# Attention matmuls on the full 128x128 tile, and memory transposes for two heads at once, in an attention-plus-MLP kernel

## The chip, the cores and the metric

The kernel runs on one core of a Trainium2 chip. The metric is device time in microseconds (us) of one execution. A core has five engines that matter here: PE (TensorE: a weight load, in the profile PEld, followed by a matmul that streams the other operand past the weights), DVE (VectorE), ACT (ScalarE), POOL (GpSimd) and SP (SyncE, whose queue issues all DMAs of this kernel). Each engine executes its own queue of instructions strictly in the order in which the program wrote them; the queues meet at semaphores.

A matmul uses a tile of the array of rows*columns: rows is the length of the contraction (the partitions of both operands), columns is how many columns of weights are loaded. The profile writes this tile as 128*128, 64*128 (64 rows), 128*64 (64 columns) or 64*64.

## The reference

Attention for B, H, S, D = 4, 8, 576, 64, followed by two MLP layers on all 2304 tokens:

```
local   = softmax(causal(q k^T / 8)) v                      # 576 x 64 for each head
q_p     = elu(q) + 1
mem_out = (q_p M_prev) / (q_p z_prev + 1e-6)                # memory part, 576 x 64 for each head
attn    = g * mem_out + (1 - g) * local,  g = sigmoid(beta[h])
x       = attn, heads side by side: 2304 x 512
x       = (s * relu(x w_in)^2 + b) w_out                    # layer 1, d_ff = 2048
out     = leaky(x w_in2; alpha) w_out2                      # layer 2, d_ff = 2048
```

## The kernel before

**Stages.** Attention goes batch by batch (b = 0 to 3) and in a batch by pairs of heads (p = 0 to 3). A head's 576 queries are five chunks, `CHUNKS`: 64, 128, 128, 128, 128 queries; a chunk of index c sees 64 + 128c keys, so its last block of keys has 64, the others 128. Chunks 0 to 2 are one set, chunks 3 and 4 the other (`SETS`). For each chunk, `scores` (L469) computes the scores on PE (L627 or L673/L674), adds the mask and finds the maximum on DVE (L497), takes the exponential on ACT (L505); `turn` (L523) splits the weights into two float16 parts (ACT L551, DVE L555), sets the padding behind the last key to zero (POOL L559) and transposes them by a DMA (SP L564); `products` (L567) multiplies the transposed weights with the values (PE L584) into the bank `ob`.

**Two kinds of batch.** Batches 0 and 1 (`EXACT`) run `pair` (L609): float32 scores, and the products of the two heads go to rows 0 to 63 and 64 to 127 of one bank, so each product loads 64 columns of weights. Batches 2 and 3, the second half, run `head` (L655) twice for each pair: scores from float32r parts with two products (L673, L674), and value products with 128 columns (the high and the low part of the values), whose two halves of the bank are added at the end.

**Memory part.** `features` (L431) computes it for a pair of heads, queries on partitions, into the slot `sa` (PE L454, DVE L459 to L463). `remembered` (L589) transposes it on PE by a product with the identity matrix (L598) into the bank of the products. In `pair` it does so for both heads at once (128 columns); in `head` for the one head (64 columns), after the head's products of that set. Chunk 0 has 64 queries, so L598 uses 64 rows there. One float32 product of the program is two matmul instructions in the profile.

**End of a set in a head.** ACT scales one half of the bank into the output tile `xt` (L695), DVE adds the other half (L697). When both heads of a pair are through, `xt` goes to DRAM as `x1` (SP L719).

**Layers.** Layer 1 works on seven blocks of tokens (512, 320, 320 and four of 288), layer 2 on eight of 288. A block reads its rows of `x1` (SP L890, split by ACT L896 and DVE L898), and for each of 16 slices of d_ff does 12 matmuls of the first product (L800 to L802), the activation (ACT L814, L815, L822, DVE L823) and 12 of the second (L834 to L836). Block 0 needs batch 0, blocks 1 and 2 need batch 1, blocks 3 and 4 batch 2, blocks 5 and 6 batch 3. Blocks 0 to 4 are what PE can do beside the attention of batches 1 to 3.

**What sets the order.** `Plan` (L62) collects all operations with their reads, writes, priorities and written-out durations; `order` (L112) makes a list schedule: each engine takes the most urgent operation that is ready, attention (`ATT`) ahead of the layers (`MOE`). The result is one fixed queue for each engine. The written-out durations (`t_f`, `t_b`, `t_r`) depend on the streamed columns and not on the tile. Tenants of the pool of 15 slots (`Slot`) take a place when so many others are free as their reserve (`RES`) asks. Banks: from batch 1 on, scores, features and the like take S0 and S1 in turn (`next_bank`), products have the single bank O.

Of the kernel before, what the change touches and what calls it, by code (L numbers as in the profile page):

```python
# [18 lines left out]
# tokens of the blocks of the two layers: (first, tokens); layer 1's first takes both places of the operands  # L19
# [6 lines left out]
# query chunks: (first query, queries); a chunk sees the keys up to its last query  # L26
CHUNKS = [(0, 64), (64, 128), (192, 128), (320, 128), (448, 128)]
SETS = [(0, 1, 2), (3, 4)]
# chunks whose weights are transposed together
GROUPS = [[(0,), (1, 2)], [(3,), (4,)]]  # L30
NC = len(CHUNKS)
# [22 lines left out]
class Slot:  # L54
    """A tenant of the pool of equal slots; it gets its place when the operations are ordered."""
# [6 lines left out]
class Plan:  # L62
    """Operations in a logical order with what they read and write. order() is a list schedule
    of the graph: every engine takes, of the operations that are ready, the most urgent. A slot
    is taken by its first operation, if as many more are free as the slot's reserve asks, and
    is free again after its last."""
# [38 lines left out]
    def either(self, ways, **kw):  # L105
        """An operation for whichever of the engines comes to it first: ways is {engine: (duration, function)}."""
        eng = next(iter(ways))
        i = self.op(eng, *ways[eng], **kw)
        if len(ways) > 1:
            self.ways[i] = ways  # L110

    def order(self):  # L112
# [32 lines left out]
        def spot(t, s):  # L145
            """Where a slot could go: the last extra place, or else the one that has been free for longest."""
# [12 lines left out]
        while len(out) < n:  # L159
# [50 lines left out]
            if e == "PE":  # L210
                # at half the clock unless the last tick was busy enough
# [58 lines left out]
def build(tc, kd, kz, qd, vd, qp, mzd, beta8, sb2, win1, wout1, win2, wout2, alpha, outT):  # L270
# [7 lines left out]
    with tc.tile_pool(name="sb", bufs=1) as sb, tc.tile_pool(  # L278
# [5 lines left out]
        # the parts of a slice of d_ff: w_in's and w_out's; before they are there, the last slices' room serves as slots  # L284
# [13 lines left out]
        def cut(t, n, k, step=None):  # L298
            """The first n elements of the k-th part of t."""
            return t[:, k * (step or n):k * (step or n) + n]  # L300
# [27 lines left out]
        def at(s, n, dt=F32):  # L328
            """The first n elements of a slot, as dt."""
# [12 lines left out]
        # the last 128 columns: -8e9 where the key lies after the query  # L342
# [7 lines left out]
        def consts():  # L350
            # wsc = (1 + exp(beta)) / LIFT = 1 / ((1 - g) LIFT); bgc = 1 + exp(-beta) = 1 / g
            A.activation(out=wsc, in_=bsc, func=AF.Exp)
            A.activation(out=bgc, in_=bsc, func=AF.Exp, scale=-1.0)
# [14 lines left out]
        # the banks of MoE products serve the first batch's attention  # L368
# [8 lines left out]
        def gate(hg, ahead, ahead0):  # L377
            """A load for a head waits for the scores of an earlier one."""
# [3 lines left out]
        def either(kind, a_dur, a_fn, d_dur, d_fn, **kw):  # L382
            """An operation for the scalar or, of the kinds in FLEX, also for the vector engine."""
# [10 lines left out]
        # They are scaled by LIFT over the sum of their magnitudes, so that no part leaves float16's range.  # L394
        def values(b, p):
# [19 lines left out]
            # un = 1 / (scale LIFT)  # L415
# [53 lines left out]
        def scores(b, h, g, keys, scored):  # L469
            """keys: what the products read; scored: (rows, columns) -> the product's instructions."""  # L470
# [4 lines left out]
            for c in cs:  # L475
# [4 lines left out]
                # keys in one or two banks: (bank, column of maximum and sum, first key, keys)  # L480
# [10 lines left out]
                for bk, col, k0, kn in parts_s:  # L491
                    sp = bank_of[bk][0:nq, 0:kn]
                    dur, mm = scored(sp, q0, nq, k0, kn)
# [20 lines left out]
            # rows 64.. of chunk 0's column were set once and stay finite  # L514
# [8 lines left out]
        def turn(b, g, group, parts, turned):  # L523
            """group: what is transposed together, (head of the pair, chunk)."""
# [13 lines left out]
            for pw, c in group:  # L538
# [19 lines left out]
                # what is transposed with the chunk's last 64 keys has to be something; nothing uses it  # L558
# [8 lines left out]
        def products(g, part, parts, turned, sf, obk, ok, high, rows, first=False):  # L567
            """The products with the values: part (head of the pair, chunk) into rows of the bank. high: the high and
            low parts of the values go to the same rows, else the low ones follow in the next 64."""
# [6 lines left out]
            def mm():  # L576
                P = p_t()
                W = at(sf, 2 * NKB * 2 * D, FP16).rearrange("p (n h e) -> p n h e", h=2, e=2 * D)
                for kb in range(nkb):
                    kk = min(128, nk - kb * 128)  # L580
                    cols = [(slice(0, D), kb), (slice(D, 2 * D), kb), (slice(0, D), nkb + kb)] if high else [
                        (slice(0, 2 * D), kb), (slice(0, 2 * D), nkb + kb)]
                    for w, x in cols:
                        T.matmul(obk[rows, q0 - o0:q0 - o0 + nq], W[0:kk, kb, pw, w], P[0:kk, x, 0:nq],  # L584
# [4 lines left out]
        def remembered(g, heads, sa, obk, ok, rows, ch, first=True):  # L589
            """The memory part, transposed into the bank."""  # L590
# [3 lines left out]
            def mm():  # L594
                for c in cs:
                    q0, nq = CHUNKS[c]
                    F = at(sa, 2 * D * NC).rearrange("p (c e) -> p c e", c=NC)[0:nq, c, heads]
                    T.matmul(obk[rows, q0 - o0:q0 - o0 + nq], F, ident[0:nq, 0:nq], start=(first and c == cs[0]), stop=False,  # L598
# [402 lines left out]
```

## Time and profile before

| | us |
|---|---|
| median of 3 runs (lowest, highest) | 1096.52 (1095.52, 1099.56) |
| span of the profiled execution | 1099.4 |
| PE busy in it | 1073.4 (98%) |
| DVE busy | 684.6 (62%) |
| ACT busy | 529.8 (48%) |
| attention of batches 0 and 1, beside it block 0 from 105 on | 0 to 257 |
| attention of batches 2 and 3, beside it blocks 1 to 4 | 257 to 568 |
| rest of layer 1, layer 2 | 568 to 1099 |

The profile lists no device time of the profiled execution apart from its span, which lies at the upper end of the three runs. A PE line of the timeline gives the start of its first matmul, the time from there to the end of its last one, the line of the kernel, the tile, the form of the streamed operand and how many follow each other. Matmuls overlap, so what one costs in the queue is the time from its start to the start of the next line, not its own duration.

### The profile page before, as it was taken

To read this page: it belongs to the slowest core of one execution; us is meant where nothing else is said; L and a number is where in the kernel's file an instruction comes from. 1 tells how busy PE (TensorE), PEld (TensorE's weight loads), DVE (VectorE), ACT (ScalarE), POOL (GpSimd) and SP (SyncE) were. 2 spreads that over 40 slices of the span, in tenths; PEclk is the share of its full clock that TensorE was granted. 3 is DMA by queue.
4 is the path that set the end of the run, shared out by engine and by line. 5 is a ranking of instruction groups with operands and counts; after the bars stand their busy time and mean duration, and the time that the engine had idled before them with its cause. 6 is when DMAs were issued, how large, how long until landed. Compare 5 with 4: busy or idle time off the path is not lost.

```text
span 1099.4 us, 20528 instructions
## 1 busy us (share of the span) xinstructions
PE 1073.4 (98%) x7776; PEld 976.4 (89%) x7776; DVE 684.6 (62%) x1812; ACT 529.8 (48%) x1325; POOL 32.2 (3%) x171
## 2 busy tenths in 40 slices
PE   7978999999999999999999999999999999999998
PEld 5755777777889989989999999999999999999998
DVE  6768888867575566566646179984545454545443
ACT  7764666558576667668654466331212121212111
POOL 1100000000000000000000000000000000000000
PEclk9987999999999999999999999999999999999999
DMA  8899686665644564454434055321101010100000
GB/s 211 162 182 259 203 182 192 181 141 167 134 72 125 132 135 109 118 125 106 96 105 154 1 185 193 129 73 32 44 1 44 1 44 1 44 1 22 1 22 23
DMA packets 163860, 114.10 MB, mean 104 GB/s; under 512 B 127408, under 2 KB 141744, under 8 KB 163760
## 3 DMA queue, kind: packets, MB, share of 16 engines
q1 hardware_dynamic: 163760, 112.78, 39.1%
q8 instruction: 61, 1.00, 0.4%
q14 instruction: 39, 0.32, 0.1%
HBM read 68.19 MB, written 14.16 MB: 75 GB/s over the span
## 4 chain that ended last, share of the span: by engine, by line
PE 88%; DMA 5%; DVE 2%; issue 2%; ACT 2%; SPq 0%; POOL 0%; DVEq 0%; POOLq 0%; ACTq 0%
PE yb L834 12%; PE yb L836 12%; PE yb L835 12%; PE hb L800 8%; PE hb L802 7%; PE hb L801 7%; PE ob L584 7%; PE sp L800 3%; PE sp L801 3%; PE sp L802 3%; PE ob L598 2%; PE sp L627 2%; DMA pool<-pool 2%; PE ob L802 2%; PE ob L800 2%
## 5 line engine op out<-in xcount | busy, mean ns | idle before, releaser
L834 PE MATMUL yb<-gr,wt 128*128 128x288 f32 (+3 forms) x960 | 299.0, 311 | 0.9 <-ACT gr L822 0.9
L835 PE MATMUL yb<-gr,wt 128*128 128x288 f32 (+3 forms) x960 | 291.7, 304 | 0.0
L836 PE MATMUL yb<-gr,wt 128*128 128x288 f32 (+3 forms) x960 | 291.6, 304 | 0.0
L822 ACT CAST gr<-gt 128x288 fp32r<-128x288 f32 (+2 forms) x240 | 107.4, 447 | 305.4 <-DVE gt L820 297.0
L823 DVE TENSOR_TENSOR gr<-gt,gr 128x288 fp32r<-128x288 f32 (+2 forms) x240 | 114.2, 476 | 139.1 <-ACT gr L822 138.6
L800 PE MATMUL hb<-xr,wt 128*128 128x288 f32 (+2 forms) x576 | 186.1, 323 | 1.7 <-ACT gt L814 1.7
L834 PEld LDWEIGHTS yb<-gr,wt 128*128 128x128 f32 x960 | 181.0, 189 | 7.6 <-issue 2.1
L836 PEld LDWEIGHTS yb<-gr,wt 128*128 128x128 f32 x960 | 181.3, 189 | 3.6 <-DVE gr L823 0.8
L835 PEld LDWEIGHTS yb<-gr,wt 128*128 128x128 f32 x960 | 180.9, 188 | 2.0 <-issue 0.2
L802 PE MATMUL hb<-xr,wt 128*128 128x288 f32 (+2 forms) x576 | 178.6, 310 | 0.0
L801 PE MATMUL hb<-xr,wt 128*128 128x288 f32 (+2 forms) x576 | 178.6, 310 | 0.0
L800 PEld LDWEIGHTS hb<-xr,wt 128*128 128x128 f32 x576 | 108.8, 189 | 8.6 <-ACT gt L814 2.6
L801 PEld LDWEIGHTS hb<-xr,wt 128*128 128x128 f32 x576 | 109.0, 189 | 2.9 <-issue 0.6
L802 PEld LDWEIGHTS hb<-xr,wt 128*128 128x128 f32 x576 | 108.9, 189 | 3.0
L814 ACT ACTIVATE gt<-hb 128x288 f32<-128x288 f32 (+2 forms) x112 | 49.7, 444 | 106.8 <-PE hb L802 105.8
L505 ACT ACTIVATE pool<-sp,mx 64x64 f32<-64x64 f32 (+2 forms) x153 | 72.4, 474 | 35.4 <-DVE mx L497 27.2
L584 PEld LDWEIGHTS <-pool 64*64 64x64 f16 (+3 forms) x930 | 55.1, 103 | 38.1 <-issue 19.7
L497 DVE CUSTOM_DVE_ANT_0 sp<-sp,mask 64x64 f32<-64x64 f32 (+4 forms) x132 | 56.5, 438 | 42.6 <-PE sp L674 26.5
L584 PE MATMUL ob<-pool 128*128 128x128 f16 (+5 forms) x855 | 76.8, 221 | 4.1 <-DMA pool<-pool 4.0
L800 PE MATMUL sp<-xr,wt 128*128 128x288 f32 x256 | 75.5, 295 | 0.0
L801 PE MATMUL sp<-xr,wt 128*128 128x288 f32 x256 | 75.5, 295 | 0.0
L802 PE MATMUL sp<-xr,wt 128*128 128x288 f32 x256 | 75.4, 295 | 0.0
(174 smaller groups left out, 1694.1 us busy)
## 6 DMA issues: line engine op xcount, KB each, us to landing
pool<-win SPq DMA_DIRECT2D x19, 512.0 KB, 4.4
pool<-wout SPq DMA_DIRECT2D x17, 512.0 KB, 4.5
room<-wout SPq DMA_DIRECT2D x15, 512.0 KB, 4.3
room<-win SPq DMA_DIRECT2D x13, 512.0 KB, 4.3
pool<-qd SPq DMA_DIRECT2D x16, 288.0 KB, 3.1
pool<-kd SPq DMA_DIRECT2D x16, 288.0 KB, 3.7
pool<-y SPq DMA_DIRECT2D x16, 288.0 KB, 3.4
out_t<-pool SPq DMA_DIRECT2D x32, 144.0 KB, 1.8
```

What stands on the lines that cost most here:

```text
L497: op("DVE", t_dve(kn, 1.04, 0 if mk is None else 60), lambda sp=sp, nq=nq, mo=mo, kn=kn, mcol=mcol, last=last: V.tensor_tensor_reduce(out= ...
L505: op("ACT", t_act(kn, 50, 180), lambda sp=sp, p_c=p_c, k0=k0, kn=kn, mcol=mcol, scol=scol: A.activation(out=p_c()[:, k0:k0 + kn], in_=sp, ...
L584: T.matmul(obk[rows, q0 - o0:q0 - o0 + nq], W[0:kk, kb, pw, w], P[0:kk, x, 0:nq], start=(first and kb == x == 0), stop=False, skip_group_c ...
L800: T.matmul(H_, W_h, X_h, start=(d == 0), stop=False)
L801: T.matmul(H_, W_h, X_l, start=False, stop=False)
L802: T.matmul(H_, W_l, X_h, start=False, stop=(d == KD - 1))
L814: op("ACT", t_act(n, 50), lambda: A.activation(out=t_, in_=H_, func=AF.Relu), r=[hk, "gr"], w=[tk], prio=-1)
L822: op("ACT", t_act(n), lambda: A.copy(out=G_h, in_=t_), r=[tk], w=[("gh", gj)], prio=-1)
L823: op("DVE", t_dve(n), lambda: V.tensor_tensor(out=G_l, in0=t_, in1=G_h.bitcast(F32), op=ALU.subtract), r=[tk, ("gh", gj)], w=[("gl", gj)], ...
L834: T.matmul(Y, W_h, G_h, start=(f == 0), stop=False)
L835: T.matmul(Y, W_l, G_h, start=False, stop=False)
L836: T.matmul(Y, W_h, G_l, start=False, stop=(f == KF - 1))
```

## The change

Four edits, and the priorities that go with them (the diff also blanks comments, which moves nothing up to L490):

1. Chunk 0's scores load 128 columns of weights (queries 0 to 127) in place of 64; rows 64 to 127 of the result are not read.
2. The products with the last block of keys use all 128 rows; the padding is zero.
3. `remembered` uses all 128 rows, also for chunk 0, and always both heads.
4. In batches 2 and 3 `remembered` leaves `head`. A new `recall` does it once for each pair, ahead of the pair's scores, in a bank of the ring S0/S1, and ACT or DVE (whichever the schedule finds free) scales the result into `xt`. At the end of a set `head` then adds both halves of its bank to `xt` with two DVE operations; the ACT operation L695 is gone.

```diff
 # scores
+                    dur, mm = scored(bank_of[bk][:, 0:kn], q0, k0, kn)
                     sp = bank_of[bk][0:nq, 0:kn]
-                    dur, mm = scored(sp, q0, nq, k0, kn)
...
 # products
-                    kk = min(128, nk - kb * 128)
...
-                        T.matmul(obk[rows, q0 - o0:q0 - o0 + nq], W[0:kk, kb, pw, w], P[0:kk, x, 0:nq],
+                        T.matmul(obk[rows, q0 - o0:q0 - o0 + nq], W[:, kb, pw, w], P[:, x, 0:nq],
                                  start=(first and kb == x == 0), stop=False, skip_group_check=True)
...
-        def remembered(g, heads, sa, obk, ok, rows, ch, first=True):
+        def remembered(g, sa, obk, ok, prio):
...
-                    F = at(sa, 2 * D * NC).rearrange("p (c e) -> p c e", c=NC)[0:nq, c, heads]
-                    T.matmul(obk[rows, q0 - o0:q0 - o0 + nq], F, ident[0:nq, 0:nq], start=(first and c == cs[0]), stop=False,
+                    F = at(sa, 2 * D * NC).rearrange("p (c e) -> p c e", c=NC)[:, c]
+                    T.matmul(obk[:, q0 - o0:q0 - o0 + nq], F, ident[:, 0:nq], start=(c == cs[0]), stop=False,
                              skip_group_check=True)
...
 # pair
-                            T.matmul(sp, at(sqp, S)[:, q0:q0 + nq], at(s, S)[:, k0:k0 + kn], start=True, stop=True)
+                            T.matmul(sp, at(sqp, S)[:, q0:q0 + 128], at(s, S)[:, k0:k0 + kn], start=True, stop=True)
...
+        def recall(b, p, sa, xt):
+            j = p % 2
+            for g in range(len(SETS)):
+                ok = next_bank(b, "S")
+                obk = bank_of[ok]
+                remembered(g, sa, obk, ok, ATT + cnt["ch"] * 10 - 4)
+                o0, qn = span_of(g)
+                either("x", t_act(qn, 50, 93), lambda o0=o0, qn=qn, obk=obk: A.activation(
+                    out=at(xt, S)[:, o0:o0 + qn], in_=obk[:, 0:qn], func=AF.Copy, scale=vsc[:, j, 1:2]),
+                    t_dve(qn, 1.04, 60), lambda o0=o0, qn=qn, obk=obk: V.tensor_scalar(
+                    out=at(xt, S)[:, o0:o0 + qn], in0=obk[:, 0:qn], scalar1=vsc[:, j, 1:2], scalar2=None, op0=ALU.mult),
+                    r=[ok, ("un", j)], w=[(xt, odd, g) for odd in range(2)])
...
 # head
-                    T.matmul(sp, qh[:, q0:q0 + nq], ks[:, k0:k0 + kn], start=True, stop=False)
-                    T.matmul(sp, ql[:, q0:q0 + nq], ks[:, k0:k0 + kn], start=False, stop=True)
+                    T.matmul(sp, qh[:, q0:q0 + 128], ks[:, k0:k0 + kn], start=True, stop=False)
+                    T.matmul(sp, ql[:, q0:q0 + 128], ks[:, k0:k0 + kn], start=False, stop=True)
...
-                remembered(g, slice(D * odd, D * odd + D), sa, obk, ok, slice(r0, r0 + 64), ch0, False)
...
-                op("ACT", t_act(qn, 50, 93), lambda xr=xr, qn=qn, obk=obk: A.activation(
-                    out=xr(), in_=obk[r1:r1 + 64, 0:qn], func=AF.Copy, scale=un[r0:r0 + 64]), r=[ok, ("un", j)], w=[(xt, odd, g)])
-                op("DVE", t_dve(qn, 1.04, 60), lambda xr=xr, qn=qn, obk=obk: V.scalar_tensor_tensor(
-                    out=xr(), in0=obk[r0:r0 + 64, 0:qn], scalar=un[r0:r0 + 64], in1=xr(),
-                    op0=ALU.mult, op1=ALU.add), r=[("un", j)], w=[ok, (xt, odd, g)])
+                for r, w in ((r1, []), (r0, [ok])):
+                    op("DVE", t_dve(qn, 1.04, 60), lambda xr=xr, qn=qn, obk=obk, r=r: V.scalar_tensor_tensor(
+                        out=xr(), in0=obk[r:r + 64, 0:qn], scalar=un[r0:r0 + 64], in1=xr(),
+                        op0=ALU.mult, op1=ALU.add), r=[ok, ("un", j)], w=w + [(xt, odd, g)])
...
 # attention
-                    head(b, 2 * p, sa, sf, xt)
-                    head(b, 2 * p + 1, sa, sf, xt)
+                    recall(b, p, sa, xt)
+                    head(b, 2 * p, sf, xt)
+                    head(b, 2 * p + 1, sf, xt)
```

## Rows read from the trace of the kernel before

**Rows 1.** Stretches: length, busy us of PE, PEld, DVE, ACT, POOL, clock, DMA.

```profile
0.00:105.00 105.00, 87.67 (x606) 60.31 (x606) 78.88 (x296) 73.32 (x207) 10.15 (x59) 0.91 0.88 202
105.00:257.00 152.00, 151.27 (x877) 112.80 (x878) 121.08 (x320) 93.72 (x217) 7.29 (x32) 0.99 0.70 186
257.00:568.00 311.00, 308.01 (x2329) 277.95 (x2328) 193.73 (x588) 217.30 (x573) 14.77 (x80) 1.00 0.48 112
```

**Rows 2.** Waits in 257:568: who waited for whom, us in total, times, longest.

```profile
ACT gt L814 <- PE hb L802: 44.3, 35, 3.5
DVE sp L497 <- PE sp L674: 32.5, 41, 2.3
```

**Rows 3.** What L584 in 257:568 waited for: us, times.

```profile
  DMA pool<-pool: 2.0, 5
```

**Rows 4.** PE timeline, a head of batch 2, first set: start us, us, what.

```profile
310.16 0.31 PE L835 MATMUL yb<-gr,wt 128*128 128x322 f32 x1
310.30 0.30 PE L836 MATMUL yb<-gr,wt 128*128 128x322 f32 x1
310.54 0.23 PE L584 MATMUL ob<-pool 64*128 64x64 f16 x2
310.70 0.41 PE L800 MATMUL hb<-xr,wt 128*128 128x320 f32 x1
310.95 0.31 PE L801 MATMUL hb<-xr,wt 128*128 128x320 f32 x1
...
312.56 0.19 PE L673 MATMUL sp<-ks,qh 128*64 128x64 f32 x1
...
312.93 1.04 PE L584 MATMUL ob<-pool 128*128 128x128 f16 x10
313.91 0.91 PE L598 MATMUL ob<-ident,pool 64*64 64x64 f32 x6
314.75 0.42 PE L834 MATMUL yb<-gr,wt 128*128 128x322 f32 x1
```

**Rows 5.** PE timeline, the same head's chunk 4 and its memory part.

```profile
319.23 0.84 PE L584 MATMUL ob<-pool 128*128 128x128 f16 x10
320.00 0.65 PE L598 MATMUL ob<-ident,pool 128*64 128x128 f32 x4
320.58 0.40 PE L673 MATMUL sp<-ks,qh 128*128 128x288 f32 x1
```

**Rows 6.** The first seven matmuls of that chunk 4, all on the full tile.

```profile
319.23 0.56 PE L584 MATMUL ob<-pool 128*128 128x128 f16 x7
```

**Rows 7.** PE timeline in batch 1: memory transposes of both heads, full tile.

```profile
152.80 0.61 PE L598 MATMUL ob<-ident,pool 128*128 128x128 f32 x4
153.16 0.48 PE L800 MATMUL hb<-xr,wt 128*128 128x512 f32 x1
153.47 0.40 PE L801 MATMUL hb<-xr,wt 128*128 128x512 f32 x1
```

**Rows 8.** PE timeline in batch 1: chunk 4's products and what follows.

```profile
165.14 1.14 PE L584 MATMUL ob<-pool 128*64 128x128 f16 x15
166.21 0.50 PE L800 MATMUL hb<-xr,wt 128*128 128x512 f32 x1
```

**Rows 9.** The first twelve of those products, those with 128 rows.

```profile
165.14 0.86 PE L584 MATMUL ob<-pool 128*64 128x128 f16 x12
```

**Rows 10.** L697 in 257:568: length, DVE busy us, clock, DMA share, GB/s.

```profile
257.00:568.00 311.00, 15.98 (x31) 1.00 0.48 112
```

**Rows 11.** Form group in 257:568: products on the full tile: busy us, mean ns.

```profile
L584 PE MATMUL ob<-pool 128*128 128x128 f16 x320 | 28.9, 221 | 1.4 <-DMA pool<-pool 1.4
```

**Rows 12.** The last DMA into x1: start us, us, what.

```profile
568.99 0.33 SPq L719 DMA_DIRECT2D x<-pool  x1
```

**Rows 13.** The split of block 5's input, the first block after attention.

```profile
574.45 0.83 DVE L898 TENSOR_TENSOR xr<-pool,xr 128x288 fp32r<-128x288 f32 x2
```

**Rows 14.** The first matmul of block 5 on PE.

```profile
583.46 0.29 PE L800 MATMUL hb<-xr,wt 128*128 128x288 f32 x1
```

More of the change, by code (lines that the diff above doesn't have):

```diff
@@ L596, in mm @@
                     q0, nq = CHUNKS[c]
-                    F = at(sa, 2 * D * NC).rearrange("p (c e) -> p c e", c=NC)[0:nq, c, heads]
-                    T.matmul(obk[rows, q0 - o0:q0 - o0 + nq], F, ident[0:nq, 0:nq], start=(first and c == cs[0]), stop=False,
+                    F = at(sa, 2 * D * NC).rearrange("p (c e) -> p c e", c=NC)[:, c]
+                    T.matmul(obk[:, q0 - o0:q0 - o0 + nq], F, ident[:, 0:nq], start=(c == cs[0]), stop=False,
                              skip_group_check=True)
-            op("PE", sum(t_f(CHUNKS[c][1]) for c in cs), mm, r=[(sa, g), "ident"], w=[ok], prio=ATT + ch * 10)
+            op("PE", sum(t_f(CHUNKS[c][1]) for c in cs), mm, r=[(sa, g), "ident"], w=[ok], prio=prio)
         def span_of(g):
@@ L624, in pair, with scored @@
                 for odd in range(2):
-                    def scored(sp, q0, nq, k0, kn, s=sk[odd]):
+                    def scored(sp, q0, k0, kn, s=sk[odd]):
                         def mm():
-                            T.matmul(sp, at(sqp, S)[:, q0:q0 + nq], at(s, S)[:, k0:k0 + kn], start=True, stop=True)
+                            T.matmul(sp, at(sqp, S)[:, q0:q0 + 128], at(s, S)[:, k0:k0 + kn], start=True, stop=True)
                         return t_f(kn), mm
@@ L637, in pair @@
                             turn(b, g, [(odd, c) for c in group], parts, turned)
-                remembered(g, slice(0, 2 * D), sa, obk, ok, slice(0, 128), ch0)
+                remembered(g, sa, obk, ok, ATT + ch0 * 10)
                 for odd in range(2):
@@ L652, in pair, with head @@
                     r=[ok, ("un", j)], w=[(xt, odd, g) for odd in range(2)])
-        def head(b, h, sa, sf, xt):
+        def recall(b, p, sa, xt):
[10 more added lines that the diff above has]
+                    r=[ok, ("un", j)], w=[(xt, odd, g) for odd in range(2)])
+        def head(b, h, sf, xt):
             hg = b * H + h
@@ L669, in head, with scored @@
                 out=ql, in0=at(sq, S), in1=qh.bitcast(F32), op=ALU.subtract), r=[sq, "qh"], w=["ql"])
-            def scored(sp, q0, nq, k0, kn):
+            def scored(sp, q0, k0, kn):
                 def mm():
-                    T.matmul(sp, qh[:, q0:q0 + nq], ks[:, k0:k0 + kn], start=True, stop=False)
-                    T.matmul(sp, ql[:, q0:q0 + nq], ks[:, k0:k0 + kn], start=False, stop=True)
+                    T.matmul(sp, qh[:, q0:q0 + 128], ks[:, k0:k0 + kn], start=True, stop=False)
+                    T.matmul(sp, ql[:, q0:q0 + 128], ks[:, k0:k0 + kn], start=False, stop=True)
                 return 2 * t_r(kn), mm
```

## The prediction

> **What bounds the kernel now.** I read the busy shares by stretch first [rows 1]. From 257 to 568, the attention of batches 2 and 3, PE is busy 308.0 of 311 us, ACT 217.3, DVE 193.7. Busy time on PE does not by itself prove a bound, since matmuls overlap, so I looked next at who waits for whom there. ACT waited 44.3 us for the first product of the layers and DVE 32.5 us for scores [rows 2]; PE waited 2.0 us in all, five times, for the transposed weights [rows 3]. The queues are fixed, and PE's is the one that the others stand behind. Third, the PE timeline, start to start: what a switch of tile costs. From 105 to 257 PE is busy 151.3 of 152, DVE 121.1. From 0 to 105 PE is busy 87.7, its clock averages 0.91, so it ran in part at the lower of its two levels (1.2 and 2.4 GHz), and it waits there for loads and transposes [rows 1].
>
> **Prices.** A layer matmul of 322 columns takes 0.14 to 0.15 us from start to start from 310.16 to 310.30 [rows 4]. A float16 product on the full tile takes (0.56 - 0.22) / 6 = 0.057, the length of one being 0.22 [rows 6, 11]. A float32 transpose on the full tile: four of them and one 512-column matmul took 0.67; the latter is 0.147 x 512/320 = 0.235, so 0.11 each [rows 7]. That is twice what a 128-column float16 step takes, so I use 0.11 also where a short matmul is followed by a float32 load on the full tile.
>
> A change of tile shows up at two places. The piece with the other tile starts late: 310.30 to 310.54 is 0.24 instead of 0.15. And after the return the first matmul takes 310.70 to 310.95, 0.25 instead of 0.15, because its weights were not loaded in advance [rows 4]. So one excursion costs some 0.2 us beside its own work.
>
> **Batches 2 and 3, one head.** All its matmuls end on 128*128, so every switch goes.
> - Chunk 0's products, with the matmul ahead and the one behind: 310.30 to 310.95 is 0.65 [rows 4]; without switches 0.15 + 0.03 + 0.11 + 0.15 = 0.44. Gain 0.21.
> - Chunks 1 and 2 together: 312.93 to 313.91 is 0.98 for ten; 9 x 0.057 + 0.11 = 0.62. Gain 0.36.
> - First set's memory part: 313.91 to 314.75 is 0.84, and 0.10 on its successor. It leaves the head: 0.94.
> - Chunk 4: 319.23 to 320.00 is 0.77, becomes 0.62. Gain 0.15. Chunk 3, which returns to the layers by itself, is taken as the same and 0.10 for its successor: 0.25.
> - Second set's memory part: 320.00 to 320.58 is 0.58, and 0.10 behind it: 0.68 [rows 5].
>
> Together 2.59 us. Against it: `recall` issues ten float32 instructions of 0.11 for a pair, 0.55 for each head, beside full-tile work on both sides. Chunk 0's scores load 128 columns in place of 64: four instructions took 312.56 to 312.93, 0.37 [rows 4]. Full-tile scores of 64 columns are not in the trace; bounded by 0.03 (half a float16 step) and 0.11 (the float32 transpose) each, I take 0.11, since the weights are as large as there: 0.44, a loss of 0.07. Net 2.59 - 0.55 - 0.07 = 1.97 us, for 16 heads **31.5 us** of PE time.
>
> One thing in the trace could speak against the wider tile. The Trainium skill, TensorEngine Tiling, section Theoretical Speedup, says that contractions of up to 64 rows can run up to twice as fast on row tiles, which would make padding to 128 rows a loss. By that rule the last blocks, two products in each of 5 chunks, would cost half a step each or 16 x 5 x 0.057 = 4.6 us more than I count. Nothing here has that gain: a ten with two 64-row products took 0.77 where ten full steps give 0.57 [rows 5, 6].
>
> **The other engines in that stretch.** ACT loses 32 evictions, DVE gets 32 more of 16.0 / 31 = 0.52 us, 16.5 in all [rows 10]. `recall` adds 16 evictions on either engine, some 0.5 each by the same row, 8 us. DVE then has 194 + 16.5 + up to 8 = 211 to 218 us in a stretch of about 285: 74 to 77%, covered. No DMA and nothing on POOL is moved; SP sees `xt` written at the same end. New waits: a pair's first scores stand behind `recall`'s eviction in the ring S0/S1, and behind those scores the layers' matmuls in PE's queue; the first half of a set's end now makes DVE, not ACT, wait for the products, and behind it stand L497 and L823, for which scores' exponentials and second products wait. `recall` comes right after `features`, ahead of the pair's burst of scores, so I cost it at nothing; without that cover it is one PE piece and one eviction, about 1 us for each of 8 pairs.
>
> What is late next? The chain scores, DVE, ACT, transpose, products was overtaken by PE only five times; with PE a tenth faster it will be more often. No row gives the slack of each. Bounds: 0, and the whole 31.5 less what is left to do behind attention (second rival). I take 7 us, about a fifth, near the lower end, since the waits of ACT and DVE for PE (44.3 + 32.5) are larger than the gain [rows 2].
>
> **Batches 0 and 1.** The products stay on 128*64; only the inner switch to 64*64 goes. Fifteen products of chunk 4 took 165.14 to 166.21, 1.07; the twelfth began 0.86 - 0.22 = 0.64 in, so the end took 0.43 [rows 8, 9, 11]. Without the inner switch: 3 x 0.057 and the way back to the full tile, which I put at 0.15 (a step and the 0.1 of a switch; bounds 0.11 and the 0.58 - 3 x 0.11 = 0.25 of rows 5). Gain 0.11. For a batch: 32 such chunks 3.5, chunk 2 following chunk 1 directly 8 x 0.11 = 0.9, chunk 0's scores 8 x 0.2 = 1.6 (two switches and an exposed load less larger loads), chunk 0 in four memory parts 4 x 0.3 = 1.2: 7.2 us. In batch 1 PE is full and only block 0 can fill it, with DVE at 121 of 152 [rows 1]: I take 6 (0 to 7.2). In batch 0 PE waits for others: I take 3 (0 to 7.2); where its clock falls may move, 3 us either way.
>
> **Sum.** 31.5 - 7 + 6 + 3 = 33.5 us. The profiled span is 1099.4, 2.9 above the median of 1096.5; the terms are absolute, so I take them off both: span 1066, time **1063 us**.
>
> **Rivals.**
> *Attention keeps its pace.* If pairs of batches 2 and 3 are paced by slots, loads and DVE/ACT, PE finishes blocks 1 to 4 early and idles. The last `x1` is issued at 569.0, block 5's input is split at 575.3 and its first matmul runs at 583.5, so 8 us of cover and then 516 us to the end [rows 12 to 14]. With the 9 us of batches 0 and 1 the last `x1` is at 560 and the end 560 + 6.3 + 516 = 1082 of span, 1079 in time. For it: one pool of slots, one bank O. Against: rows 2 and 3.
> *Slower.* `recall` takes `xt` before the pair's scores instead of at the first set's end, and the ring S0/S1 serves two more tenants. If the 15 slots then delay the next pair's loads, each pair gets longer. From the same sum, the end passes 1099.4 when the last `x1` comes after 577: 17 us later than 560, 2.1 us for each of 8 pairs, which now take 311 / 8 = 39 us [rows 1]. At 4 us a pair: 592 + 522 = 1114 span, 1111. Against: `sa` is free right after `recall`, so the slots even out.
> *No give-back.* All of PE's time comes back and batch 0 follows: 31.5 + 7.2 + 7.2 = 46: 1051.
>
> **How the numbers follow.** Forecast (1055 to 1072) 0.70, no give-back (about 1050) 0.12, pace kept (about 1079) 0.13, slower 0.05. The range reaches over the second and third: 1049 to 1081. A measurement of this kernel tells about 0.5%, 5.5 us, from no change. Faster by more: 0.93; the same, a kept pace without the gain ahead of it: 0.03; slower: 0.04.
>
> **What would show it.** In the profile after: no 64*128, 64*64 or 128*64 in 257 to 568; L598 there x80 in place of x160; start-to-start steps of 0.057 through a whole chunk; PE still over 97% busy; block 5's first matmul near 550. I am wrong if L584 waits for transposes by tens of us, if PE idles ahead of block 5, or if a pair of batches 2 and 3 still takes 39 us.

## The result, and the profile after

The kernel after takes **1062.18 us** (median of 4 runs, 1059.52 to 1065.86), the kernel before 1097.54 in the same comparison (1095.52 to 1099.56): a ratio of 0.9674, 95% interval 0.9646 to 0.9702. Forecast were 1063 us and a range from 1049 to 1081. The span of the profiled execution is 1061.6 us.

Some lines have moved: L497 is now L498, L673/L674 are L687/L688, L697 is L709, L719 is L732, L800 to L802 are L813 to L815, L814 is L827, L834 to L836 are L847 to L849; L584, L598 and L627 stand where they were. `recall` evicts in L662 (ACT) or L664 (DVE).

Stretches first. I cut all kernels at the same three events, which any trace shows: the first matmul of block 0 (batch 0 is through), of block 1 (batch 1 is through) and of block 5 (batch 3 is through). Each row: stretch, length, busy us of PE, PEld, DVE, ACT and POOL with their instructions, granted clock, DMA share, GB/s. Before:

```profile
0.00:104.90 104.90, 87.57 (x606) 60.21 (x606) 78.78 (x296) 73.22 (x206) 10.15 (x59) 0.91 0.88 202
104.90:254.80 149.90, 149.17 (x862) 110.74 (x862) 119.92 (x313) 92.12 (x214) 7.29 (x32) 0.99 0.70 185
254.80:583.50 328.70, 325.71 (x2460) 295.61 (x2460) 203.73 (x614) 226.72 (x595) 14.77 (x80) 1.00 0.49 119
583.50:1099.40 515.90, 510.97 (x3853) 509.84 (x3852) 282.13 (x593) 137.69 (x314) 0.00 (x0) 1.00 0.15 51
```

After:

```profile
0.00:99.30 99.30, 81.38 (x605) 60.43 (x605) 78.27 (x294) 72.47 (x204) 10.22 (x59) 0.90 0.93 213
99.30:241.90 142.60, 140.77 (x864) 108.99 (x862) 120.08 (x315) 92.78 (x214) 7.44 (x32) 1.00 0.75 196
241.90:545.30 303.40, 295.77 (x2380) 287.29 (x2379) 221.15 (x648) 216.02 (x577) 14.99 (x80) 1.00 0.54 126
545.30:1061.60 516.30, 511.00 (x3854) 509.88 (x3852) 281.62 (x592) 137.69 (x314) 0.00 (x0) 1.00 0.16 52
```

The last stretch is the same to 0.4 us, so everything was won before block 5: 5.6 us in batch 0, 7.3 in batch 1, 25.3 in batches 2 and 3. In the third row PE's busy time fell by 29.9 us, and its idle time (length less busy) rose from 3.0 to 7.6. DVE gained 17.4 us of work and ACT lost 10.7; neither became the bound.

The PE timeline of a head of batch 2 answers to [rows 4, 5]; read it start to start:

```profile
293.94 0.31 PE L815 MATMUL hb<-xr,wt 128*128 128x320 f32 x1
294.09 0.23 PE L584 MATMUL ob<-pool 128*128 128x64 f16 x2
294.16 0.40 PE L813 MATMUL hb<-xr,wt 128*128 128x320 f32 x1
294.39 0.31 PE L814 MATMUL hb<-xr,wt 128*128 128x320 f32 x1
...
296.47 0.19 PE L687 MATMUL sp<-ks,qh 128*128 128x64 f32 x1
296.50 0.27 PE L688 MATMUL sp<-ks,ql 128*128 128x64 f32 x1
296.61 0.34 PE L687 MATMUL sp<-ks,qh 128*128 128x192 f32 x1
296.78 0.28 PE L688 MATMUL sp<-ks,ql 128*128 128x192 f32 x1
296.89 0.33 PE L847 MATMUL yb<-gr,wt 128*128 128x322 f32 x1
...
297.35 0.73 PE L584 MATMUL ob<-pool 128*128 128x128 f16 x10
297.89 0.39 PE L847 MATMUL yb<-gr,wt 128*128 128x322 f32 x1
298.12 0.31 PE L848 MATMUL yb<-gr,wt 128*128 128x322 f32 x1
```

Chunk 0 with its neighbours takes 293.94 to 294.39, 0.45 (0.44 worked out; 0.65 before). The ten products of chunks 1 and 2 take 0.54, on average 0.054 each; their successor takes 0.23 (297.89 to 298.12) in place of 0.15, and these 0.08 more make the 0.62 worked out. The four scores take 296.47 to 296.89, 0.42 (0.44 worked out). `recall` in the same view:

```profile
277.71 0.83 PE L598 MATMUL sp<-ident,pool 128*128 128x64 f32 x6
278.29 0.40 PE L847 MATMUL yb<-gr,wt 128*128 128x322 f32 x1
278.52 0.31 PE L848 MATMUL yb<-gr,wt 128*128 128x322 f32 x1
```

The first set's six transposes take 0.58, with 0.08 on their successor (0.23 in place of 0.15); the second set's four take 0.36 (279.78 to 280.14), with as much behind them. That is 0.11 an instruction, the price taken from [rows 7]. The groups by form from 241.9 to 545.3 (busy us, mean ns, then idle time ahead and what ended it) show L598 80 times (before 160), everything on 128*128, and where PE idled:

```profile
L584 PE MATMUL ob<-pool 128*128 128x128 f16 x448 | 32.9, 220 | 4.3 <-DMA pool<-pool 3.9 <-DVE mx L498 0.2
L598 PE MATMUL sp<-ident,pool 128*128 128x128 f32 x64 | 10.4, 285 | 0.0
L584 PE MATMUL ob<-pool 128*128 128x64 f16 x32 | 3.7, 197 | 2.8 <-DMA pool<-pool 2.5 <-DVE nrm L459 0.3
L598 PE MATMUL sp<-ident,pool 128*128 128x64 f32 x16 | 2.9, 260 | 0.1
```

7.1 of the 7.6 us of idle time stand ahead of L584, 6.4 of them ended by the DMA that brings the transposed weights. What L584 (with its weight loads) waited for, answering to [rows 3], and who waited for whom, answering to [rows 2]:

```profile
  DMA pool<-pool: 8.7, 10
```

```profile
ACT gt L827 <- PE hb L815: 46.1, 37, 3.0
DVE sp L498 <- PE sp L688: 22.3, 32, 2.7
DVE pool L709 <- PE ob L584: 13.4, 14, 1.6
```

So transposes are overtaken ten times instead of five, for 8.7 us instead of 2.0. DVE's wait for scores fell from 32.5 to 22.3; DVE now also waits at the set's end for the products, 13.4 us, where before ACT had waited 21.3 us for PE (L695 for L598); and ACT waits for the layers' first product as before. Last, the end of the attention, answering to [rows 12, 14]:

```profile
529.82 0.33 SPq L732 DMA_DIRECT2D x<-pool  x1
...
545.16 0.30 PE L849 MATMUL yb<-gr,wt 128*128 128x288 f32 x1
545.30 0.29 PE L813 MATMUL hb<-xr,wt 128*128 128x288 f32 x1
```

The last `x1` leaves 39.2 us earlier, block 5 starts 38.2 us earlier, and PE goes into it from the matmul before without a gap: blocks 1 to 4 still cover the way.

### The profile page after: what moved, and what is told of

It reads as the page before. It is cut to its first block, busy times and chain, and to the rows that moved or that the text cites. A ratio compares the mean times of both kernels' runs of the same rounds, so it can differ in the third digit from the quotient of the medians.

```text
span 1061.6 us, 20391 instructions
## 1 busy us (share of the span) xinstructions
PE 1028.9 (97%) x7696; PEld 966.6 (91%) x7696; DVE 701.1 (66%) x1846; ACT 519.0 (49%) x1307; POOL 32.6 (3%) x171
## 4 chain that ended last, share of the span: by engine, by line
PE 59%; DMA 3%; issue 1%; DVE 1%; ACT 1%; SPq 0%; POOL 0%; POOLq 0%; ACTq 0%; DVEq 0%
PE yb L847 10%; PE yb L849 9%; PE yb L848 9%; PE hb L813 5%; PE hb L815 4%; PE hb L814 4%; PE sp L813 3%; PE sp L815 3%; PE sp L814 3%; DMA pool<-pool 3%; PE ob L815 2%; PE ob L813 2%; PE ob L814 2%; PE ob L584 1%; PE sp L687 0%
## 5 line engine op out<-in xcount | busy, mean ns | idle before, releaser
L847 PE MATMUL yb<-gr,wt 128*128 128x288 f32 (+3 forms) x960 | 299.2, 312 | 0.6 <-ACT gr L835 0.5
L849 PE MATMUL yb<-gr,wt 128*128 128x288 f32 (+3 forms) x960 | 291.6, 304 | 0.0
L836 DVE TENSOR_TENSOR gr<-gt,gr 128x288 fp32r<-128x288 f32 (+2 forms) x240 | 114.3, 476 | 112.7 <-ACT gr L835 111.9
L813 PE MATMUL hb<-xr,wt 128*128 128x288 f32 (+2 forms) x576 | 185.2, 322 | 1.4 <-ACT gt L827 1.4
L847 PEld LDWEIGHTS yb<-gr,wt 128*128 128x128 f32 x960 | 181.1, 189 | 4.2 <-ACT gr L835 1.3
L849 PEld LDWEIGHTS yb<-gr,wt 128*128 128x128 f32 x960 | 181.4, 189 | 3.5 <-DVE gr L836 0.6
L815 PE MATMUL hb<-xr,wt 128*128 128x288 f32 (+2 forms) x576 | 177.9, 309 | 0.0
L814 PE MATMUL hb<-xr,wt 128*128 128x288 f32 (+2 forms) x576 | 177.9, 309 | 0.0
L813 PEld LDWEIGHTS hb<-xr,wt 128*128 128x128 f32 x576 | 108.5, 188 | 5.9 <-ACT gt L827 2.3
L814 PEld LDWEIGHTS hb<-xr,wt 128*128 128x128 f32 x576 | 108.7, 189 | 2.8 <-issue 0.6
L815 PEld LDWEIGHTS hb<-xr,wt 128*128 128x128 f32 x576 | 108.5, 188 | 2.9
L827 ACT ACTIVATE gt<-hb 128x288 f32<-128x288 f32 (+2 forms) x112 | 49.7, 444 | 100.3 <-PE hb L815 99.5
L584 PEld LDWEIGHTS <-pool 128*128 128x128 f16 (+1 forms) x930 | 55.0, 105 | 31.2 <-issue 22.9
L498 DVE CUSTOM_DVE_ANT_0 sp<-sp,mask 128x320 f32<-128x320 f32 (+4 forms) x132 | 56.7, 436 | 29.4 <-PE sp L688 18.5
L813 PE MATMUL sp<-xr,wt 128*128 128x288 f32 x256 | 75.5, 295 | 0.0
L814 PE MATMUL sp<-xr,wt 128*128 128x288 f32 x256 | 75.5, 295 | 0.0
L815 PE MATMUL sp<-xr,wt 128*128 128x288 f32 x256 | 75.4, 295 | 0.0
L584 PE MATMUL ob<-pool 128*128 128x128 f16 (+3 forms) x855 | 63.6, 220 | 10.1 <-DMA pool<-pool 9.4
```

The source lines that it names most:

```text
L498: op("DVE", t_dve(kn, 1.04, 0 if mk is None else 60), lambda sp=sp, nq=nq, mo=mo, kn=kn, mcol=mcol, last=last: V.tensor_tensor_reduce(out= ...
L584: T.matmul(obk[rows, q0 - o0:q0 - o0 + nq], W[:, kb, pw, w], P[:, x, 0:nq], start=(first and kb == x == 0), stop=False, skip_group_check=True)
L813: T.matmul(H_, W_h, X_h, start=(d == 0), stop=False)
L814: T.matmul(H_, W_h, X_l, start=False, stop=False)
L815: T.matmul(H_, W_l, X_h, start=False, stop=(d == KD - 1))
L827: op("ACT", t_act(n, 50), lambda: A.activation(out=t_, in_=H_, func=AF.Relu), r=[hk, "gr"], w=[tk], prio=-1)
```

## Experiments

Two theories stood against each other. **Tile changes:** what was won is the changes of tile that PE no longer makes, about 0.2 us each, and besides them the 80 transposes fewer that `recall` needs for two heads at once; as much of it comes off the time as the attention's other waits let through. **Order:** the new queues (`recall` early, other ends of a set) moved work together better, or the waits set the pace, and the tile is by the way.

### x_rows: edit 2 alone

```diff
-                    kk = min(128, nk - kb * 128)
-                        T.matmul(..., W[0:kk, kb, pw, w], P[0:kk, x, 0:nq],
+                        T.matmul(..., W[:, kb, pw, w], P[:, x, 0:nq],
```

> The kernel before with one edit: the products with the last block of keys use 128 rows (edit 2 alone). The queues keep the order of before on every engine. Theory A, a change of tile costs about 0.1 us on the way out and 0.1 to 0.2 on the way back: in a head the rows of before give 0.21 (chunk 0) + 0.32 (chunks 1 and 2) + 0.25 (chunk 3) + 0.11 (chunk 4) = 0.89 us, 14 us for 16 heads; batch 1 gains 4.4 us, batch 0 about 2; together some 19 us, time about 1078. Rival B, the gain comes from the new order of the queues, or from the memory part: no change, 1097. Rival C, row tiles of 64 save time and padding loses it: 1100 or more.

Measured: 1080.27 us, ratio 0.9858 (0.9834 to 0.9882), near the 1078 of theory A. The order of all queues is that of before. The stretch of batches 2 and 3:

```profile
244.40:559.80 315.40, 311.89 (x2459) 294.08 (x2458) 203.46 (x613) 225.86 (x595) 14.77 (x80) 1.00 0.50 123
```

13.3 us shorter than before with the same queues: no order can have done that. Per head it is 0.83 us; PE's busy time fell by 13.8.

### x_switch: before, with more changes of tile

The same products, but in each chunk first all of the one part, then all of the next, so that the short block of keys comes up once in each pass.

```diff
-                for kb in range(nkb):
+                for y, kb in [(y, kb) for y in range(3 if high else 2) for kb in range(nkb)]:
...
-                    for w, x in cols:
+                    for w, x in cols[y:y + 1]:
```

> The kernel before with the same matmuls, shapes and counts, and the same order of everything else; only inside a chunk's products the loop over high and low parts is the outer one, so that the last block of keys, on 64 rows, comes two times (batches 2 and 3) or three times (batches 0 and 1) by itself instead of once together. Theory A: 64 chunks of heads get two more changes of tile, 0.2 us each chunk, 13 us; 32 chunks of batch 1 get four more, 0.45 us, 14 us; batch 0 the same on paper, of which perhaps half shows: 7 us. Time about 1131. Rival, the cost is in the small shapes themselves, not in the change: 1097.

Measured: 1142.56 us, ratio 1.0427 (1.0392 to 1.0461), above theory A's 1131, since batch 0 grew by more than the 7 us put there. Its stretches:

```profile
0.00:119.80 119.80, 109.45 (x606) 69.60 (x606) 78.20 (x294) 73.40 (x205) 10.15 (x59) 0.84 0.78 178
119.80:282.70 162.90, 162.17 (x862) 115.71 (x862) 120.55 (x315) 92.22 (x214) 7.28 (x32) 0.99 0.65 171
282.70:623.90 341.20, 338.71 (x2459) 301.28 (x2458) 203.59 (x613) 226.69 (x595) 14.81 (x80) 1.00 0.47 113
```

In batches 2 and 3 each of the 4 x 16 chunks with more than one block gets one excursion more: 64, for 12.5 us, 0.195 each. In batch 1 each of 4 x 8 chunks gets two more: 64, for 13.0 us, 0.20 each. One number, twice. The same chunks of the head in [rows 4, 5], in the PE timeline of x_switch:

```profile
341.23 1.46 PE L584 MATMUL ob<-pool 128*128 128x128 f16 x10
342.62 0.91 PE L598 MATMUL ob<-ident,pool 64*64 64x64 f32 x6
...
348.16 1.05 PE L584 MATMUL ob<-pool 128*128 128x128 f16 x10
349.13 0.65 PE L598 MATMUL ob<-ident,pool 128*64 128x128 f32 x4
```

Chunks 1 and 2 take 1.39 where they took 0.98 (two more excursions, 0.41), chunk 4 takes 0.97 where it took 0.77. The matmuls are the same in number, shape and work. The Trainium skill, TensorEngine Tiling, section Key Properties, says that a change of the tiling mode drains the engine. This trace agrees in that the change costs time, and puts 0.20 us on the way out and back; that draining is what takes this time, no view here shows. Batch 0 grew by 14.9 us. PE's busy time rose there by 21.9, its idle time fell by 7.0 (17.3 to 10.4). The same 64 excursions explain 12.8 of the 21.9; the other 9 went with a lower clock, 0.84 on average against 0.91 before.

### x_pair and x_recall: the first half alone, the recall alone

x_pair has edits 1 to 3 in batches 0 and 1 and nothing in 2 and 3:

```diff
+                    kk = 128 if high else min(128, nk - kb * 128)
...
+                    kq = 128 if first else nq
...
+                            T.matmul(sp, at(sqp, S)[:, q0:q0 + 128], at(s, S)[:, k0:k0 + kn], start=True, stop=True)
```

> The kernel before with edits 1 to 3 in batches 0 and 1 alone; batches 2 and 3 as before. Theory A with the sum of the prediction: 6 us in batch 1 and 3 in batch 0, 1088; block 1 of the layers, which started at 254.8, starts 9 us sooner, and from there on nothing changes. The profile after had this start at 241.9, 13 us sooner, which would give 1084. Rival, batch 0 waits for transposes and batch 1 for DVE, so that nothing shows: 1096.

Measured: 1087.06 us, ratio 0.9919 (0.9901 to 0.9937).

x_recall is the kernel after with the products and scores of before: only `recall`, on full tiles, and the new end of a set are left.

```diff
+                    kk = min(128, nk - kb * 128)
...
+                    kq = 128 if full else nq
...
-                    T.matmul(sp, qh[:, q0:q0 + 128], ks[:, k0:k0 + kn], start=True, stop=False)
+                    T.matmul(sp, qh[:, q0:q0 + nq], ks[:, k0:k0 + kn], start=True, stop=False)
```

> The kernel before with the memory part of batches 2 and 3 moved into one transposition for each pair (edit 4, on the full tile); chunk 0's scores, and the products with 64 rows, as before. Theory A: 0.94 + 0.68 leave each head, 0.55 comes back, and two ways back to the full tile of 0.10 stay with the products: 0.87 us, 14 us for 16 heads of PE time, some 3 of it lost in new waits: about 1086. Rival, the move itself matters more than PE's time, by a freer ACT and a shorter end of a set: 1075 or less. Rival, recall's bank and its early output tile hold the pairs up: 1095 or more.

Measured: 1086.99 us, ratio 0.9915 (0.9891 to 0.994). The third stretch of either, x_pair first:

```profile
241.90:569.60 327.70, 325.37 (x2459) 295.57 (x2458) 203.55 (x613) 226.54 (x595) 14.77 (x80) 1.00 0.49 119
```

```profile
253.50:570.00 316.50, 312.10 (x2379) 288.67 (x2378) 221.42 (x648) 216.48 (x577) 15.03 (x80) 1.00 0.51 121
```

x_pair leaves batches 2 and 3 where they were to 1.0 us, and x_recall takes 12.2 us off them. With 13.3 of x_rows that makes 25.5; the kernel after has 25.3. In PE's busy time the parts are 13.8 and 13.6, together 29.9, 2.5 more: the way from the products to the memory part and back costs a change of tile so long as one of the two is left on a narrow one. Idle time rose by 4.6 us with both together and by 0.5 and 1.4 with the parts, 2.7 more, and takes that again. So the parts add up, and order has no share of its own that could be seen. The 12.2 us of x_recall are not tile alone, though: they hold the 80 transposes that it no longer issues. x_double, next, tells the two apart.

### x_double and x_four: the transposes of recall two and four times

```diff
-                for c in cs:
+                for c in cs * times:
```

`times` is 2 and 4 where `recall` calls. The planner's durations are as in after, so the order is too; only PE gets more to do, by 80 and 240 transposes of 0.11 us.

> The changed kernel with the memory transposes of batches 2 and 3 issued twice (the second pass may add to the first in chunks other than a set's first, so the memory part is changed there); every queue keeps its order. PE gets 80 more float32 transposes of 0.11 us, 8.8 us. Theory A, PE paces the pairs of batches 2 and 3: the time rises by 5 to 9 us (PE waits 7.6 us there in all, a part of which the extra work can fill), to 1067 to 1071. Rival, the pairs are paced by transposes, slots and DVE, and PE has air: 1062 to 1064.

> The changed kernel with the memory transposes of batches 2 and 3 issued four times (the later passes may add to the first in chunks other than a set's first, so the memory part is changed there); every queue keeps its order. PE gets 240 more of 0.11 us, 26.4 us. Issued twice, 8.8 us of them made the stretch from block 1 to block 5 2.7 us longer and took 5.1 us out of PE's waits there (7.6 to 2.5). Theory A, PE paces the pairs and its waits are what the chain falls behind by: the waits are used up, and all but some 6 us show: the stretch becomes 303.4 + 20 = 323, the time about 1082. Rival, the pairs are paced by the chain and PE has further air in the order of its queue: less than half shows, 1075 or less.

Measured: x_double 1065.56 us, ratio 0.9715 (0.9699 to 0.9731), between its two expectations and with an interval that still touches that of the kernel after, so that it is read by its stretch; x_four 1084.51, ratio 0.9899 (0.9867 to 0.9931), near the 1082 expected. Their third stretches:

```profile
239.50:545.60 306.10, 303.59 (x2459) 296.01 (x2458) 221.14 (x648) 215.41 (x577) 14.93 (x80) 1.00 0.51 126
```

```profile
240.40:565.80 325.40, 321.37 (x2620) 313.76 (x2618) 221.28 (x648) 215.24 (x577) 14.92 (x80) 1.00 0.49 118
```

8.8 us of new work made the stretch 2.7 us longer, and PE's idle time fell from 7.6 to 2.5: the first 5 us filled waits. 26.4 us made it 22.0 longer. PE therefore still sets the pace of batches 2 and 3, and about 5 us of what it was relieved of went into waiting for transposes. The forecast had put 7 us there.

x_double also shows what the tile is worth, order having no share that could be seen. It has as many matmuls in this stretch as before (2459, before 2460), among them all 160 transposes, but all on the full tile, and yet the stretch is 22.6 us shorter than before and PE 22.1 us less busy. The 80 transposes that `recall` saves are the other 7.8 of the 29.9 us of PE's work, and 2.7 of the 25.3 us of the stretch: so about three quarters of the work won is tile, and the rest is matmuls that are no longer issued.

### x_late: the planner reckons transposes 0.6 us later

If the ten waits for transposes come from an order that expects them too soon, a later due time should move other matmuls ahead of them.

```diff
-                done[i] = dma_free + 900.0
+                done[i] = dma_free + (900.0 if dur < 500 else 1500.0)
```

> The changed kernel, but the schedule reckons with transposes that land 0.6 us later, so PE's queue holds more of the layers' matmuls between scores and products. Theory A: what the sum lost to new waits (PE waits 7.6 us between block 1 and block 5, against 3.0 before, most of it for transposes) comes from products that stand in PE's queue at the very moment at which the transposes land; moved back, PE waits 3 us or less, and the time falls by up to 4 us, to 1058. Rival, the pairs are paced by the chain itself: later products delay the next pair, no gain or a loss, 1062 to 1066.

Measured: 1068.92 us, ratio 0.9744 (0.9722 to 0.9766), 7 us more than the kernel after and above both expectations. Batch 1, then batches 2 and 3:

```profile
99.90:250.30 150.40, 143.39 (x869) 109.28 (x867) 121.90 (x317) 93.95 (x218) 6.85 (x36) 0.99 0.73 188
250.30:553.90 303.60, 298.99 (x2388) 290.43 (x2389) 215.70 (x641) 212.13 (x571) 14.92 (x80) 0.99 0.52 119
```

In batches 2 and 3 PE's idle time fell by 3.0 us, its busy time rose by 3.2, and the stretch is as long as in the kernel after (303.6 against 303.4); it holds 8 matmuls more, which had moved in from elsewhere. Batch 1 became 7.8 us longer, 5 of them idle time of PE. One constant in the plan does not win the waits back; that theory falls. Whether another order could win the 5 us is open.

### x_scores: chunk 0's scores on 64 columns again

The kernel after without its edit 1 (`q0:q0 + 128` is `q0:q0 + nq` again in both places).

> The changed kernel with chunk 0's scores on 64 columns again (edit 1 undone), the queues in the same order. By start-to-start steps of the profile after, the full tile costs a head of batches 2 and 3 about 0.05 us (four score matmuls 0.42 against 0.37), so 0.8 us are won back there; in batches 0 and 1 the two changes of tile come back, 0.2 us a head, 1.6 in batch 1 and as much on paper in batch 0. Time 1063 to 1065. If a change of tile to 64 columns costs float32r scores as much as it does float32 scores, batches 2 and 3 lose 3 us instead: 1067.

Measured: 1065.08 us, ratio 0.971 (0.9695 to 0.9724); the interval overlaps with that of the kernel after. Batch 1, then batches 2 and 3:

```profile
101.60:245.20 143.60, 141.99 (x864) 108.39 (x862) 120.56 (x318) 92.74 (x214) 7.38 (x32) 1.00 0.74 195
245.20:547.70 302.50, 294.95 (x2379) 286.42 (x2378) 221.03 (x648) 215.58 (x577) 14.99 (x80) 1.00 0.53 126
```

The stretch of batches 2 and 3 is 0.9 us shorter than with the edit (0.07 a head, 1.1, had been forecast as its cost); batch 1 is 1.0 longer, where 1.6 had been forecast. In batches 2 and 3 the edit costs that little, in batch 1 it gains as little.

### x_full, x_vx and x_slots13: no narrow tile at all, and what it costs in room

In batches 0 and 1 the kernel after still has its products on 64 columns. x_full gives each head's values 64 columns of zeros beside them, so that these products take 128*128 and add zero to the other head's half. That needs a tile of its own for the values, and so two slots of the ring less.

```diff
-NSLOT = 15
+NSLOT = 13
+        vx = sb.tile([128, 2 * VX], F32, name="vx")
...
+                            T.matmul(obk[:, q0 - o0:q0 - o0 + nq], W[:, kb, y, pw * D:pw * D + 2 * D], P[:, x, 0:nq],
```

x_vx has the same room, slots and order, but products on 64 columns (`obk[rows, ...]`, `W[:, kb, y, 2 * pw * D:2 * pw * D + D]`). x_slots13 is the kernel after with 13 slots and nothing else.

> The changed kernel with the float16 products of batches 0 and 1 on the full tile as well: the values lie in a tile of their own with 64 zero columns between the two heads, so that each product loads 128 columns, 64 of them zero, and adds nothing to the other head's rows; 13 slots in place of 15, since the values take none. Theory A: no change of tile is left in the program. Between block 0's and block 1's first matmul the changed kernel still spends 7.8 us of PE in changes: 6 to 8 us less there, and some 4 of as many in batch 0: about 1051. Rival, 13 slots hold the pairs up: 1062 or more.

> The kernel with the zero-padded values and 13 slots, every queue in the same order, but the products of batches 0 and 1 load the 64 columns of their head alone (128*64), as in the changed kernel. Theory A: the missing slots and the new storage made that kernel slow (1096 against 1062), and the full tile in it still saved time: here 8 us more in batch 1 and up to 8 in batch 0, 1100 to 1112. Rival, the zero columns themselves cost what the tile saves: 1096 or less.

> The kernel after with 13 slots in the ring in place of its own number; its instructions are otherwise those of the kernel after, so only what the planner must hold back differs. Slots theory: the two missing slots made the version with 13 slots and a tile of its own for the values lose the 34 us: about 1090 to 1097 us, with TensorE idle near 12 us in batch 1, near 9 us in batches 2 and 3 and near 9 us in the blocks behind block 5's first matmul, as there. Rival, the zero-padded value tile (its two extra vector operations and the space it takes) or another order made that loss: about 1062 to 1066 us, with TensorE idle near 2 us in batch 1 and near 1 us behind block 5's first matmul.

Measured: x_full 1096.28 us, ratio 0.9997 (0.9984 to 1.0011); x_vx 1096.97, ratio 1.0009 (0.9997 to 1.002); x_slots13 1134.99, ratio 1.036 (1.0328 to 1.0393). x_full, expected at 1051 if tiles alone counted, went its rival's way. x_vx came out below the 1100 to 1112 that would have shown a saving of 8 us or more by the full tile, 0.7 us above x_full. Batch 1 of x_full, then of x_vx:

```profile
107.40:261.00 153.60, 140.84 (x861) 112.32 (x859) 111.22 (x301) 89.51 (x209) 6.99 (x36) 0.94 0.63 166
```

```profile
106.10:262.70 156.60, 142.88 (x861) 112.04 (x859) 112.47 (x303) 89.76 (x210) 6.75 (x36) 0.96 0.62 165
```

PE idles 12.8 and 13.7 us there, where the kernel after idles 1.8. The full tile made batch 1 of x_full 3.0 us shorter than that of x_vx, batches 2 and 3, where the two do the same, are 4.0 longer (310.0 against 306.0; why is open), and the times agree within their intervals. So the version without any narrow tile is no gain: in the same room its tile does not move the time, and with that room it is 34 us behind the kernel after. x_slots13, all four stretches:

```profile
0.00:109.10 109.10, 77.42 (x575) 60.35 (x576) 82.99 (x291) 69.37 (x191) 9.19 (x52) 0.86 0.87 206
109.10:283.40 174.30, 156.90 (x892) 119.32 (x891) 120.86 (x319) 95.07 (x223) 7.65 (x39) 0.91 0.59 153
283.40:607.30 323.90, 304.29 (x2394) 293.11 (x2392) 219.53 (x642) 217.98 (x576) 14.85 (x80) 0.97 0.47 111
607.30:1133.50 526.20, 514.21 (x3843) 511.60 (x3840) 287.37 (x602) 136.93 (x312) 0.00 (x0) 0.99 0.16 55
```

It missed both expectations. Two slots less cost 72.8 us, twice what x_vx lost; all four stretches are longer, PE's idle time is 48.0 us larger in sum (80.7 against 32.7), the granted clock is lower in the same stretches (0.91 and 0.97 against 1.00), and PE's busy time is 23.9 us longer. That the loss is larger fits: in x_vx the values' parts no longer take slots of the ring, in x_slots13 they do. The missing slots are enough to explain what x_vx lost; that its value tile cost nothing beside them isn't shown, since no run has the tile and 15 slots.

## Why the prediction was right

- **The bound.** PE's queue set the pace of batches 2 and 3 before, and it still does: x_switch lengthens the stretch by 12.5 us for 13.0 of PE work added to before, x_four by 22.0 for 25.6 added to after.
- **31.5 us of PE time in batches 2 and 3.** Measured 29.9. The parts have their sizes: 0.62 for chunks 1 and 2, 0.45 for chunk 0, 0.42 for the scores, 0.11 a transpose. The price of an excursion, 0.2 us from one timeline, is that of x_switch (0.195 and 0.20). Its second place was misread, though. The prediction put half of the price on the first matmul after the return, 0.25 instead of 0.15 [rows 4]. Without any change of tile that matmul still takes 0.23 (294.16 to 294.39), as it does behind transposes on the full tile: it is late behind short matmuls on either tile. What went is the late start (0.24 becomes 0.15) and as much between the start of the two products and that of their successor (310.54 to 310.70 was 0.16, now 0.07). The sum came out because it put a last step of 0.11 back into the version without changes.
- **7 us for new waits.** Measured 4.6. This term was a choice between 0 and 31.5, and its size was no reading; the place was: L584 behind its transposes. Work and waits were both put a little high (1.6 and 2.4 us), so their difference, 24.5, came out as 25.3: that it lies so close is luck in part.
- **Other engines.** 64 DVE operations of L709 in place of 32, 14 evictions of `recall` on ACT and 2 on DVE: DVE +17.4 us, where 16.5 to 24.5 had been put. That `recall`'s evictions cost nothing holds: the idle time ahead of L584 leaves 0.5 us for all the rest of PE's queue.
- **Batch 1, 6 of 7.2 us.** Measured 7.3, the top of the range; x_pair, whose first two stretches are made of the same edits, 6.6. PE was full there, so the whole of it came through. In x_full and x_vx, where PE idles 13 us in batch 1, the tile of the products is worth 3.0 us there and nothing in the time.
- **Batch 0, 3 us.** The profiled stretches differ by 5.6 us, but x_recall, which changes nothing in batch 0, differs from before by 1.9 there, with the same clock. By the ratios of the times, which take 35.8 us off, less the 25.3 and 7.3 of the other stretches, 3.2 are left; x_pair's 8.9 less 6.6 and 1.0 leaves 1.3. So some 1 to 3 us is what the tile gives there; closer it can't be told, as in that stretch waits for loads and the clock move the length by as much.
- **Rivals.** *Attention keeps its pace* fell: a pair of batches 2 and 3 is 25.3 / 8 = 3.2 us shorter. *Slower* (slots) did not occur, but its mechanism is real: x_slots13, with two slots less, is 72.8 us slower. `recall`'s earlier `xt` fitted into 15 slots. *No give-back* fell by the 4.6 us of new waits.
- **The rule that spoke against it.** The Trainium skill, TensorEngine Tiling, section Theoretical Speedup, gives up to 2x for a dimension of up to 64. The prediction's estimate from it was that padding the last blocks to 128 rows would cost 4.6 us more than counted. The trace shows nothing of that cost: the padded ten take 0.54 and 0.08 on the successor, the unpadded took 0.77 and 0.98; and x_rows, which is that padding alone, is faster by 1.4%.

## What to carry to other kernels

Read matmuls start to start, and look for a group that takes longer than its count times its step: here a short product of 64 rows in between cost about 0.2 us for the way there and back, and padding it to the tile of its neighbours won that. That pays where PE is what the others wait for; in x_full, where PE idled, a full tile did not move the time. Price the neighbours' late start apart from it: a matmul behind short ones is some 0.08 us late on either tile. And before buying a wider tile with buffer space, price the space: here two slots of fifteen were worth 72.8 us, twice what the whole change won.

## What the runs showed of the hardware

- **A 64-column tile costs scores hardly anything.** Putting the float32r scores of batches 2 and 3 (L687, L688) back on 64 columns made that stretch 0.9 us shorter; with the float32 ones, batch 1 became 1.0 us longer (x_scores). Both are small against what else moves a stretch (batch 1 of x_recall, which leaves it as it was, is 0.6 us longer than before), so the sign is a hint and the smallness is the finding. The 0.2 us an excursion thus is not one price for all: it is measured here for blocks of 64 rows.
- **A step that looks like a change of tile and isn't.** The 192-column score takes 0.17 from start to start (296.61 to 296.78) on the full tile too, where a 320-column matmul takes 0.15; behind it nothing changes its tile.
- **More changes of tile went with a lower clock in batch 0.** x_switch has PE busier there than any other kernel (109.45 of 119.80 us) and yet the lowest granted clock, 0.84, that is longer at 1.2 GHz of the two levels; before has 0.91. PE's busy share and the granted clock went opposite ways. Part of that share is longer matmuls: the 54 products of L584 that go from `room` into `hb` in batch 0 have a median of 240 ns there and 219 before. No cause is shown.
- **More idle time went with a lower clock.** In x_slots13 PE idles 48.0 us more, and its busy time grew by 23.9 us with as many matmuls in all (7704, after 7703), at a granted clock of 0.91 in batch 1 where the kernel after has 1.00. That the idling lowered the clock is not shown.
